# Softmax row sums of two attention layers: the partial sums are added and inverted when the next chunk but one begins, the product comes at its fifth unit, and the seventh head group takes no weight maxima

## The chip, the cores and the metric

The kernel runs on one core of a Trainium2 chip. The metric is the device time of one execution in microseconds, as the median of several runs. A core has TensorE (PE in the profile), VectorE (DVE), ScalarE (ACT), GpSimd (POOL) and SyncE (SP), each with a queue of its own that runs in order, and 16 DMA engines that the queues of SyncE and GpSimd feed here.

## What is computed

A sequence of 2048 positions with 1024 features goes through four layers, each added to its input: attention with 32 heads, a spectral filter, and both once more. The change lies in the attention layers.

```python
def _A_ref(x, wqkv, wo):
    B, S, D = x.shape
    H = 32
    Dh = D // H
    qkv = (lambda x, *d: x.transpose(*d))((x @ wqkv).reshape(B, S, 3, H, Dh), 2, 0, 3, 1, 4)
    q, k, v = qkv[0], qkv[1], qkv[2]
    scores = jnp.einsum("bhqd,bhkd->bhqk", q, k) * (Dh ** -0.5)
    p = _softmax(scores, axis=-1)
    o = jnp.einsum("bhqk,bhkd->bhqd", p, v)
    return (lambda x, *d: x.transpose(*d))(o, 0, 2, 1, 3).reshape(B, S, D) @ wo
...
x = x + _A_ref(_layernorm(x, axis=-1), A_wqkv, A_wo)
x = x + _B_ref(_layernorm(x, axis=-1), B_w_r, B_w_i)
```

`_B_ref` multiplies the two-dimensional Fourier transform of its input by a filter and transforms back.

## The kernel before

**Tiling.** The 32 heads form eight head groups `g` of four. A group takes its 2048 queries in four chunks `c` of 512, and a chunk takes the 2048 keys in sixteen units `kt` of 128. A unit (`S`, L714) makes the scores of four heads with twelve matmuls (L720) into two of the three PSUM tiles `s`; ScalarE writes two tiles `p` of exponentials (L724); VectorE adds them to the chunk's running sum `acc` (`add`, L737: L741 for the first two units together, L743 for each later one, two instructions a unit); TensorE multiplies them by the values (`PV`, L726: L730). Two chunks alternate between two tiles `acc`, one of which lies in the tensor `R`. There are eight buffers `p`. `PV` and the adds run one or two units behind the scores: at each even `kt` the loop does the products of the last two units, and the adds follow in that round and the next; at `kt == 0` both adds of the chunk before are done at once.

**Fill work.** Between the units TensorE computes the queries, keys and values of later groups (`qk_chunk`, L411, and `v_tiles`, L468) in small pieces, into a single PSUM bank `x`. ScalarE and VectorE then empty that bank: the high half of a split by L215, the low half by L216 on VectorE, or by L472 on ScalarE for values. The next sum can only start when the bank is empty. Norms of queries and keys bound the scores: `norms` (L437) takes one of the three tiles `s`, multiplies by ones (L443) and lets VectorE take the maximum (L445); GpSimd then makes the bias of the exponentials (L449 to L456, with a reduction over partitions, L451). In the last group but one the fill work ends with the splits of the output weights (`load_wo`), and in the last group it is the output projection (`wo_part`, L545: L531 into the bank `x`, emptied by L557 on VectorE).

**Row sums.** When a chunk's `acc` is complete, at `kt == 0` of the following chunk, `partials` (L746) puts seven DMAs on GpSimd's queue. Four add the four strips of 32 partitions into a DRAM tensor `zd` (L749), two fold that tensor in halves (L752), and one loads the remaining eight partial sums into `part` (L754). Each waits for the one before. `invert_partials` (L757) then has VectorE add the eight (L759), take the reciprocal (L761) and keep its maximum for a check (L762), and SyncE store it (`zr`, L764) and load it back spread over the partitions (`zt`, four DMAs, L766). `times` (L788: L789) multiplies the chunk's output `oc` by it, and `out` (L792) splits the product into halves (L795 on ScalarE, L796 on VectorE) and stores them (`od`, L798), from where `load_o` (L520) fetches them for the projection. The last group does the same without DMAs, with a matmul and transposes (`fin`, L769).

**Order.** The loop (L823 to L892) is written out by hand. TensorE and ScalarE run in the order written (`manual_schedule`, L823). VectorE, GpSimd and SyncE are ordered by a scheduler that follows the dependences; `issue_after` ties an instruction to a given add, so that it isn't moved ahead of it. In the first layer VectorE also takes the largest magnitude of each piece of the weights (`look`, L317: L320), once a chunk at `kt == 3`, tied to an add, and in the last group with every fourth unit, not tied.

Of the kernel before, what the change touches and what calls it, by code (L numbers as in the profile page):

```python
# [107 lines left out]
NG, NCH, NKT, NST = 8, 4, 16, 6  # L108
# [110 lines left out]
def run(g):  # L219
    for _ in g:  # L220
        pass
# [106 lines left out]
def attention(nc, tc, layer, ap, xin, yd, wts, wo, cst, dram, flags):  # L328
# [151 lines left out]
    def sums(ph):  # L480
        return 8 if ph[0] == "v" else 4
# [38 lines left out]
    def load_o(c):  # L520
        osb[c] = xhl[:, 2 + c % 2]
        for i in range(2):
            nc.sync.dma_start(osb[c][:, i, 0:7], od[i, 0:7, :, c * 512:(c + 1) * 512].rearrange("g p n -> p g n"))
# [21 lines left out]
    def wo_part(c, t, dst, nd):  # L545

        x = xres(c, t)
        st = sm.tile([128, 2, 6], F32, name="st")
        for n in range(2):
            p = bank()  # L550
            m = wo_mm(p, c, t, n, range(nd))
            for _ in range(3 * nd - 1):
                next(m)
                yield
            run(m)
            sl = slice(n * 512, n * 512 + 512)
            nc.vector.scalar_tensor_tensor(dst[:, sl], p, 1.0 / (SO * SW), x[:, sl], op0=ALU.mult, op1=ALU.add)  # L557
            if nd == 8:
                nc.vector.bn_stats(st[:, n], dst[:, sl])
                if n:  # L560
                    r0 = c * 512 + t * 128
                    nc.sync.dma_start(yd[r0:r0 + 128, :], dst)
                    nc.vector.bn_aggr(mvs[:, 8 * c + 2 * t:8 * c + 2 * t + 2], st)
            yield
# [16 lines left out]
    def wo_parts():  # L581
        load_o(0)
        for t in (2, 3, 0, 1, 4, 5, 6, 7, 8, 9, 10, 11):
            if t == 8:
                two = wvp.tile([128, 2, 1024], F32, name="wv")
                wo_dst[8], wo_dst[9] = two[:, 0], two[:, 1]
            yield from wo_part(t // 4, t % 4, wo_dst[t], 8 if t == 11 else 7)
            if t in (0, 4, 9):
                load_o({0: 1, 4: 2, 9: 3}[t])

    def wo_rest(t):
        p = psS.tile([128, 2, 512], F32, name="s")
        st = wo_last(t // 4, t % 4, p, wo_dst[t], wo_dst[t], True, t < 8)
        if t < 8:
            moments.extend((wo_mean, t) if i == 0 else (wo_var, t) for i in range(2))
        else:
            nc.vector.bn_aggr(mvs[:, 2 * t:2 * t + 2], st)
# [116 lines left out]
    def S(g, c, kt):  # L714

        s = [psS.tile([128, 2, 512], F32, name="s") for _ in range(2)]
        for i, (a, b) in enumerate(((0, 0), (0, 1), (1, 0))):
            for h in range(4):
                r = slice(32 * h, 32 * h + 32)
                nc.tensor.matmul(s[h // 2][:, h % 2], K[g][r, a, kt * 128:kt * 128 + 128],  # L720
                                 Q[g][r, b, c * 512:c * 512 + 512], start=i == 0, stop=i == 2)
        for hf in range(2):
            p = P[g, c, kt, hf] = pp.tile([128, 2, 512], F32, name="p")
            nc.scalar.activation(p, s[hf], AF.Exp, bias=bias[g], scale=SCALE / (SQ * SQ))  # L724
# [32 lines left out]
    def invert_partials(g, c, part):  # L757
        z = sm.tile([128, 16], F32, name="z")
        nc.vector.tensor_reduce(z, part.rearrange("p j q -> p q j"), axis=AX.X, op=ALU.add)  # L759
        rc = sm.tile([128, 16], F32, name="rc")  # L760
        nc.vector.reciprocal(rc, z)  # L761
        nc.vector.tensor_max(flags["r"], flags["r"], rc)  # L762
        r = on.tile([128, 512], F32, name="zt")
        nc.sync.dma_start(zr[c % 2].rearrange("(p q) -> p q", q=16), rc)  # L764
        for h in range(4):
            nc.sync.dma_start(r[32 * h:32 * h + 32], zr[c % 2][512 * h:512 * h + 512].unsqueeze(0).broadcast_to([32, 512]))  # L766
        return r
# [20 lines left out]
    def times(g, c, r):  # L788
        nc.vector.scalar_tensor_tensor(r, O[g, c], SO, r, op0=ALU.mult, op1=ALU.mult)  # L789
        O[g, c] = r  # L790

    def out(g, c, eng=nc.vector):  # L792
        r = O.pop((g, c))
        t = on2.tile([128, 2, 512], F16, name="ohl")
        nc.scalar.copy(t[:, 0], r)  # L795
        eng.tensor_tensor(t[:, 1], r, t[:, 0], op=ALU.subtract)  # L796
        if g < NG - 1:
            nc.sync.dma_start(od[:, g, :, c * 512:(c + 1) * 512].rearrange("a p n -> p a n"), t)  # L798
        else:
            olast[c] = t  # L800

    pend, done, late, going, turned = [], [], [], [], []
# [6 lines left out]
    def slots(f, sums, n, steps):  # L809

        while sums:
            k = max(1, int(n / sums + 0.5))
            m = -(-steps // k)
            for i in range(0, steps, m):
                while ripe():
                    norms()
                for _ in range(min(m, steps - i)):
                    next(f, None)
                n -= 1
                yield sums - (i + m >= steps)  # L820
            sums -= 1

    with tc.manual_schedule(engines={mybir.EngineType.PE, mybir.EngineType.Activation}):  # L823
        for g in range(NG):
            todo = sum(sums(ph) for ph in beside.get(g, []))
            sl = slots(fill, todo, 22 if g == NG - 2 else 32, 24)
            wsl = slots(wof, 4, 10, 21)
            for u in range(NCH * NKT):
                c, kt = divmod(u, NKT)
                S(g, c, kt)  # L830
                if g == u == 0:
                    run(last_v)
                if kt % 2 == 0:
                    for w in pend:
                        PV(*w)
                    late = pend
                    pend = []
                    if kt == 0 and late:
                        for w in late:
                            last_add = add(*w)  # L840
                        turned, going = going, []
                        if late[1][0] == NG - 1:
                            done = [late[1][:2]]
                            fin(*done[0])
                        else:
                            going = [*late[1][:2], partials(*late[1][:2])]
                        if turned and not done:
                            with tc.issue_after(last_add.ins):
                                times(*turned)
                        late = []  # L850
                for w in late[:1]:
                    last_add = add(*w)
                late = late[1:]
                if kt == 3 and u > 3:
                    with tc.issue_after(last_add.ins):
                        wts.look()
                if kt == 11 and going:
                    with tc.issue_after(last_add.ins):
                        going[2] = invert_partials(*going)
                if kt == 3 and turned and done:  # L860
                    with tc.issue_after(last_add.ins):
                        times(*turned)
                if kt == 5 and done:
                    out(*done.pop())
                elif turned and (kt == 5 or kt == 9):
                    out(*turned[:2])
                    turned = []
                pend.append((g, c, kt))
                if kt % 2 == 0:
                    continue  # L870
                if todo:
                    todo = next(sl)
                elif g == NG - 2:
                    if left:
                        run(lwo)
                        left = 0
                    if next(wsl, None) is not None and u == NCH * NKT - 1:
                        run(wsl)
                elif g == NG - 1:
                    if u % 4 == 1:  # L880
                        wts.look()
                    if moments:
                        f, t = moments.pop(0)
                        f(t)
                    if u // 2 in rests:
                        wo_rest(rests[u // 2])
                    for _ in range(share[u // 2]):
                        next(wof)
                if g == NG - 2 and todo <= 6 and left > (8 if todo > 4 else 0):
                    next(lwo)  # L890
                    left -= 1
        for w in pend:  # L892
            PV(*w)
        for w in late + pend:
            add(*w)
        run(wof)
# [580 lines left out]
```

## Time and profile before

| | us |
|---|---|
| median of 3 runs | 3784.86 |
| lowest and highest run | 3784.84, 3788.1 |
| the profiled execution | 3787.86 |
| its span, first to last instruction | 3786.0 |
| first layer's attention up to the last chunks | 110 to 1455 |
| second layer's | 1960 to 3330 |
| mean granted TensorE clock | 0.989 |

Times in profile rows are microseconds from the span's start. A row of the timeline gives start, duration, engine, line, operation, output and inputs, how many instructions it merges, and in brackets the idle time ahead of it with the engine, tile and line that ended it. A row of the waits names who waited, for whom, the total, how many times and the longest. A row of the windows gives the stretch, its length, the busy time of PE, PEld (the weight loads), DVE, ACT and POOL, then the granted clock of TensorE as a share of full speed, the share of DMA time and GB/s. TensorE is busy when its rows say so, even if the clock is lowered; its matmuls overlap.

### The profile page before, as it was taken

How to read it: one execution, taken by the hardware profiler on the slowest of the kernel's cores; microseconds unless marked ns; L12 is line 12 of the kernel's file. 1: busy time of each engine (PE TensorE's matmuls, PEld its weight loads, DVE VectorE, ACT ScalarE, POOL GpSimd, SP SyncE). 2: the span in 40 equal slices, each digit the busy share in tenths (PEclk: the TensorE clock that was granted, in tenths of full speed). 3: DMA queues.
4: the chain of work that ended last, by engine and by line, in shares of the span. 5: the costliest groups of instructions: out<-in, count | busy, mean ns of one | idle time of the engine just before them, and what ended most of it. 6: DMA issues, size and time to landing. Idle time of an engine off the chain costs nothing.

```text
span 3786.0 us, 80539 instructions
## 1 busy us (share of the span) xinstructions
PE 3658.5 (97%) x32919; PEld 1634.9 (43%) x32919; DVE 3132.8 (83%) x3800; ACT 2932.5 (77%) x3653; POOL 638.8 (17%) x798
## 2 busy tenths in 40 slices
PE   8999999999999999999999999999999999899998
PEld 5333422343234233378963234323433432233888
DVE  7799898989898978886767888989899888688744
ACT  5778887888788867768847788878888888577686
POOL 1011111111111110014420111111111111100143
PEclk9999999999999999999999999999999999999999
DMA  6122232322232442233151232323222333421423
GB/s 193 24 51 54 50 56 44 63 42 54 43 63 49 101 98 71 79 121 121 58 162 24 51 57 49 57 43 62 41 54 51 62 58 90 101 73 68 164 88 108
DMA packets 203551, 274.33 MB, mean 72 GB/s; under 512 B 75809, under 2 KB 122529, under 8 KB 202145
## 3 DMA queue, kind: packets, MB, share of 16 engines
q1 hardware_dynamic: 164208, 195.06, 16.2%
q0 software_dynamic: 37632, 73.43, 13.7%
q8 instruction: 260, 4.26, 0.5%
q14 instruction: 123, 1.00, 0.1%
q10 hardware_dynamic: 1328, 0.59, 0.1%
HBM read 149.00 MB, written 118.42 MB: 71 GB/s over the span
## 4 chain that ended last, share of the span: by engine, by line


## 5 line engine op out<-in xcount | busy, mean ns | idle before, releaser
L724 ACT ACTIVATE p<-s,bias 128x1024 f32<-128x1024 f32 x2048 | 2169.5, 1111 | 553.8 <-PE s L720 532.1
L743 DVE TENSOR_TENSOR R<-R,p 128x1024 f32<-128x1024 f32 x896 | 1044.3, 1219 | 65.4 <-ACT p L724 63.7
L743 DVE TENSOR_TENSOR acc<-acc,p 128x1024 f32<-128x1024 f32 x896 | 1043.8, 1218 | 60.3 <-ACT p L724 58.7
L730 PE MATMUL o<-p,R 128*32 128x512 f32 x8192 | 987.1, 599 | 0.0
L411 PE MATMUL x<-big,wqk 128*128 128x512 f16 x2880 | 686.4, 384 | 37.7 <-DVE R L216 30.5
L720 PEld LDWEIGHTS <-R 32*128 32x128 f16 x12288 | 229.5, 92 | 758.0 <-issue 642.5
L411 PEld LDWEIGHTS <-wqk 128*128 128x128 f16 x3072 | 279.3, 98 | 460.1 <-issue 174.3
L730 PEld LDWEIGHTS o<-p,R 128*32 128x32 f32 x8192 | 214.1, 109 | 526.1 <-issue 526.1
L720 PE MATMUL s<-R 32*128 32x512 f16 x6144 | 428.7, 379 | 7.1 <-DVE mqk L445 6.8
L720 PE MATMUL s<-Q,R 32*128 32x512 f16 x6144 | 425.6, 377 | 9.8 <-DVE mqk L445 9.8
L468 PE MATMUL x<-wv,big 128*128 128x256 f16 x2784 | 332.1, 275 | 6.6 <-DVE R L216 4.8
L468 PEld LDWEIGHTS <-big 128*128 128x128 f16 x3072 | 292.0, 99 | 98.4 <-issue 56.5
L531 PE MATMUL x<-big 128*128 128x512 f16 x1008 | 235.7, 384 | 17.8 <-DVE R L557 17.8
L531 PEld LDWEIGHTS <-big 128*128 128x128 f16 x1428 | 135.3, 98 | 185.0 <-issue 50.6
L749 POOL DMA_DIRECT2D zd<-R x112 | 93.3, 833 | 706.3 <-DVE R L743 427.8
L749 POOL DMA_DIRECT2D zd<-acc x112 | 92.3, 824 | 709.3 <-DVE acc L743 428.7
L741 DVE SCALAR_TENSOR_TENSOR R<-p 128x1024 f32<-128x1024 f32 x64 | 75.5, 1221 | 99.0 <-ACT p L724 99.0
L752 POOL DMA_DIRECT2D zd<-zd x112 | 89.3, 798 | 397.6 <-DMA zd<-zd 174.7
L1141 DVE TENSOR_TENSOR H<-G,H 128x512 f16<-128x512 f32 (+1 forms) x68 | 46.7, 687 | 99.6 <-ACT H L1140 99.4
L741 DVE SCALAR_TENSOR_TENSOR acc<-p 128x1024 f32<-128x1024 f32 x64 | 75.8, 1221 | 44.1 <-ACT p L724 44.1
L1083 ACT COPY U<-ps 64x256 f32<-64x256 f32 (+1 forms) x272 | 97.0, 357 | 8.7 <-PE ps L1090 3.6
L1090 PE MATMUL ps<-cbi,H 128*128 128x256 f16 (+1 forms) x792 | 99.0, 273 | 3.4 <-DVE H L1141 1.9
(459 smaller groups left out, 3294.1 us busy)
## 6 DMA issues: line engine op xcount, KB each, us to landing
zd<-R POOLq DMA_DIRECT2D x112, 256.0 KB, 4.1
zd<-acc POOLq DMA_DIRECT2D x112, 256.0 KB, 4.1
wst<-in_wp SPq DMA_DIRECT2D x96, 256.0 KB, 3.5
R<-y SPq DMA_DIRECT2D x32, 512.0 KB, 6.0
w<-in_w SPq DMA_DIRECT2D x60, 256.0 KB, 2.7
zt<-zr SPq DMA_DIRECT2D x224, 64.0 KB, 2.0
od<-ohl SPq DMA_DIRECT2D x56, 256.0 KB, 2.7
big<-od SPq DMA_DIRECT2D x16, 896.0 KB, 6.9
```

Of the source, the lines that this page charges most:

```text
L411: nc.tensor.matmul(ps, a, b, start=i == 0, stop=i == 23)
L468: nc.tensor.matmul(ps[:, j], x[c][:, d, o:o + 128], w[:, n, d], start=i == 0, stop=i == 23)
L531: nc.tensor.matmul(p, a, b, start=start and d == ds[0] and i == 0, stop=stop and d == ds[-1] and i == 2)
L720: nc.tensor.matmul(s[h // 2][:, h % 2], K[g][r, a, kt * 128:kt * 128 + 128], Q[g][r, b, c * 512:c * 512 + 512], start=i == 0, stop=i == 2)
L724: nc.scalar.activation(p, s[hf], AF.Exp, bias=bias[g], scale=SCALE / (SQ * SQ))
L730: nc.tensor.matmul(O[g, c][32 * h:32 * h + 32], V[g][:, kt, 32 * h:32 * h + 32], P[g, c, kt, h // 2][:, h % 2], start=kt == 0, stop=kt == ...
L741: last_add = nc.vector.scalar_tensor_tensor(a, P[g, c, 0, hf], 1e-34, p, op0=ALU.add, op1=ALU.add)
L743: last_add = nc.vector.tensor_add(a, a, p)
L749: nc.gpsimd.dma_start(z, a[32 * j:32 * j + 32].rearrange("p a j n -> p (a j n)"), max_dma_last_dim=2048, **({"accum_op": ALU.add} if j els ...
L752: nc.gpsimd.dma_start(z[0:n], z[n:2 * n], accum_op=ALU.add, max_dma_last_dim=2048)
L1083: nc.scalar.copy(ov[64 * r:64 * r + 64, a0:a0 + m, x], tl[64 * x:64 * x + 64, :m, r])
L1090: nc.tensor.matmul(out, l, r, start=k == 0, stop=k == len(mm_) - 1)
```

## The change

The diff, cut to its core:

```diff
-            if t in (0, 4, 9):
-                load_o({0: 1, 4: 2, 9: 3}[t])
+            if t in (0, 5, 9):
+                load_o({0: 1, 5: 2, 9: 3}[t])
...
                             going = [*late[1][:2], partials(*late[1][:2])]
-                        if turned and not done:
+                        if turned:
                             with tc.issue_after(last_add.ins):
-                                times(*turned)
+                                turned[2] = invert_partials(*turned)
                         late = []
...
-                if kt == 3 and u > 3:
+                if kt == 3 and u > 3 and g < NG - 2:
                     with tc.issue_after(last_add.ins):
                         wts.look()
-                if kt == 11 and going:
-                    with tc.issue_after(last_add.ins):
-                        going[2] = invert_partials(*going)
-                if kt == 3 and turned and done:
+                if kt == 5 and done:
+                    out(*done.pop())
+                if kt == 5 and turned:
                     with tc.issue_after(last_add.ins):
                         times(*turned)
-                if kt == 5 and done:
-                    out(*done.pop())
-                elif turned and (kt == 5 or kt == 9):
+                if kt == 7 and turned:
                     out(*turned[:2])
                     turned = []
```

For a chunk that ends when the following one begins, `invert_partials` moved from unit 11 of the following chunk to the first unit of the chunk after that; `times` moved from that first unit to unit 5, `out` from unit 5 to unit 7. The third load of the output halves moved from behind the projection's fifth tile to behind its sixth. The weight maxima tied to unit 3 are dropped in the last two groups, so that those pieces are left to the untied ones of the last group. Nothing is computed differently. The orders of TensorE and GpSimd are the same as before.

The second half of the fifth head group's last chunk on VectorE. Before (`acc` is the running sum, `R` here the keys, `wqk` the next weights):

```order
L796 TENSOR_TENSOR ohl<-zt,ohl 128x512
L216 SCALAR_TENSOR_TENSOR R<-x,R 128x512
L422 TENSOR_TENSOR sq<-R 128x512
L743 TENSOR_TENSOR acc<-acc,p 128x1024 x4
L216 SCALAR_TENSOR_TENSOR wqk<-wst,wqk 128x512 x2
L743 TENSOR_TENSOR acc<-acc,p 128x1024 x4
L759 TENSOR_REDUCE z<-part 128x16
L761 RECIPROCAL rc<-z 128x16
L762 TENSOR_TENSOR fr<-fr,rc 128x16
L743 TENSOR_TENSOR acc<-acc,p 128x1024 x4
L216 SCALAR_TENSOR_TENSOR R<-x,R 128x512
```

And now, up to the next chunk's first adds:

```order
L743 TENSOR_TENSOR acc<-acc,p 128x1024 x4
L796 TENSOR_TENSOR ohl<-zt,ohl 128x512
L216 SCALAR_TENSOR_TENSOR wqk<-wst,wqk 128x512 x2
L743 TENSOR_TENSOR acc<-acc,p 128x1024 x8
L216 SCALAR_TENSOR_TENSOR R<-x,R 128x512
L422 TENSOR_TENSOR sq<-R 128x512
L743 TENSOR_TENSOR acc<-acc,p 128x1024 x8
L759 TENSOR_REDUCE z<-part 128x16
L761 RECIPROCAL rc<-z 128x16
L216 SCALAR_TENSOR_TENSOR R<-x,R 128x512
L422 TENSOR_TENSOR sq<-R 128x512
L762 TENSOR_TENSOR fr<-fr,rc 128x16
```

The three instructions of the reciprocal left the middle of the chunk and stand at its end, around a split of the keys; the subtraction L796 moved down, directly ahead of the weights' splits.

The seventh head group's second chunk on VectorE in the first layer, from its first adds (`big` holds the output weights). Before:

```order
L741 SCALAR_TENSOR_TENSOR acc<-p 128x1024 x2
L216 SCALAR_TENSOR_TENSOR R<-x,R 128x512
L216 SCALAR_TENSOR_TENSOR big<-wst,big 128x512
L320 TENSOR_REDUCE fw<-wqk 128x1
L743 TENSOR_TENSOR acc<-acc,p 128x1024 x2
L320 TENSOR_REDUCE fw<-big 128x1
L743 TENSOR_TENSOR acc<-acc,p 128x1024 x2
L216 SCALAR_TENSOR_TENSOR big<-wst,big 128x512
L743 TENSOR_TENSOR acc<-acc,p 128x1024 x4
L796 TENSOR_TENSOR ohl<-zt,ohl 128x512
L216 SCALAR_TENSOR_TENSOR big<-wst,big 128x512
L320 TENSOR_REDUCE fw<-big 128x1
```

Now:

```order
L741 SCALAR_TENSOR_TENSOR acc<-p 128x1024 x2
L216 SCALAR_TENSOR_TENSOR R<-x,R 128x512
L216 SCALAR_TENSOR_TENSOR big<-wst,big 128x512
L320 TENSOR_REDUCE fw<-big 128x1
L743 TENSOR_TENSOR acc<-acc,p 128x1024 x4
L216 SCALAR_TENSOR_TENSOR big<-wst,big 128x512
L789 SCALAR_TENSOR_TENSOR zt<-oc,zt 128x512
L743 TENSOR_TENSOR acc<-acc,p 128x1024 x4
L216 SCALAR_TENSOR_TENSOR big<-wst,big 128x512
L320 TENSOR_REDUCE fw<-big 128x1
L743 TENSOR_TENSOR acc<-acc,p 128x1024 x4
L796 TENSOR_TENSOR ohl<-zt,ohl 128x512
```

The tied maximum of `wqk` is gone from here, but untied maxima of `big` that belong to the last group stand in this group before and now.

SyncE's queue in the first head groups (`zr` and `zt` are the reciprocals' store and loads, `wst` the weights of later groups). Before:

```order
L764 DMA zr_1130<-rc 128x16
L766 DMA zt<-zr_1130 32x512 x4
L798 DMA od_132<-ohl 128x2x512
L764 DMA zr_1131<-rc 128x16
L766 DMA zt<-zr_1131 32x512 x4
L302 DMA wst<-in_wp 128x512 x4
```

Now:

```order
L764 DMA zr_1130<-rc 128x16
L766 DMA zt<-zr_1130 32x512 x4
L798 DMA od_132<-ohl 128x2x512
L302 DMA wst<-in_wp 128x512 x2
L764 DMA zr_1131<-rc 128x16
L766 DMA zt<-zr_1131 32x512 x4
L302 DMA wst<-in_wp 128x512 x2
```

Two of the weights' loads moved ahead of the store of a reciprocal.

## The prediction

> **What bounds the kernel now.** I read the page's first part, then the waits of the matmul queue (PE) in the two attention stages, then VectorE's (DVE's) waits there.
>
> ```profile
> span 3786.0 us, 80539 instructions
> PE 3658.5 (97%) x32919; PEld 1634.9 (43%) x32919; DVE 3132.8 (83%) x3800; ACT 2932.5 (77%) x3653; POOL 638.8 (17%) x798
> ```
>
> TensorE is busy for 97% of the span, so what it loses sets the time. Its waits of the first layer's attention (110 to 1455 us), then of the second's (1960 to 3330 us):
>
> ```profile
> PE x L411 <- DVE R L216: 18.6, 7, 7.3
> PE x L531 <- DVE R L557: 8.1, 1, 8.1
> PE s L720 <- DVE mqk L445: 7.8, 6, 2.5
> PE x L411 <- DVE Q L216: 4.4, 3, 3.4
> PE x L468 <- DVE R L216: 2.6, 3, 0.9
> ...
> PE x L411 <- DVE R L216: 11.9, 5, 6.1
> PE x L531 <- DVE R L557: 9.6, 1, 9.6
> PE s L720 <- DVE mqk L445: 8.8, 5, 3.3
> PE x L411 <- DVE Q L216: 1.0, 1, 1.0
> ```
>
> The columns are the total in us, the number of waits and the longest. All are waits for VectorE to empty a PSUM buffer: 41.5 us in the first layer and 31.3 in the second, 72.8 us in 32 waits. VectorE's own waits, first layer and second:
>
> ```profile
> DVE z L759 <- DMA part<-zd: 39.7, 20, 9.6
> ...
> DVE z L759 <- DMA part<-zd: 39.8, 20, 11.2
> ```
>
> VectorE stands still for 79.5 us in 40 of 56 chunks because the sum of the partial row sums (L759) comes up before its DMA has landed. The fifth head group's last chunk shows how the one makes the other; GpSimd (POOL), DVE and PE in turn:
>
> ```profile
> 949.65 4.63 POOL L451 PARTITION_ALL_REDUCE mall<-mqk  x1 [11.20 <-DVE mqk L445]
> ...
> 962.90 0.76 POOL L749 DMA_DIRECT2D zd<-R  x1
> ...
> 987.42 0.99 POOL L754 DMA_DIRECT2D part<-zd  x1 [2.25 <-DMA zd<-zd]
> ...
> 980.28 4.62 DVE L743 TENSOR_TENSOR acc<-acc,p 128x1024 f32<-128x1024 f32 x4
> 992.40 0.37 DVE L759 TENSOR_REDUCE z<-part 128x16 f32<-128x128 f32 x1 [7.50 <-DMA part<-zd]
> 992.80 0.25 DVE L761 RECIPROCAL rc<-z 128x16 f32<-128x16 f32 x1
> 993.09 0.17 DVE L762 TENSOR_TENSOR fr<-fr,rc 128x16 f32<-128x16 f32 x1
> ...
> 997.72 0.68 DVE L216 SCALAR_TENSOR_TENSOR R<-x,R 128x512 f16<-128x512 f32 x1
> ...
> 985.89 1.90 PE L411 MATMUL x<-big,wqk 128*128 128x512 f16 x8
> ...
> 998.45 3.90 PE L411 MATMUL x<-big,wqk 128*128 128x512 f16 x10 [7.29 <-DVE R L216]
> ```
>
> GpSimd was still at the bias maximum when the chunk's sums were ready, so the chain of seven DMAs began at 962.9 and ended near 991. VectorE waited 7.50 us, the split L216 behind it came late, and TensorE waited 7.29 us for that split's PSUM bank.
>
> **Part 1, the wait at L759.** The trio L759, L761, L762 moves from behind the adds of unit 9 of the following chunk to behind its last adds, six units later. Two units are four adds, 4.62 us by the row at 980.28, so the trio comes 13.9 us later or more. The longest wait is 11.2 us, so all 40 should go, 79.5 us of VectorE. GpSimd's order is unchanged, and so is TensorE's. What is late next is VectorE's plain backlog, and three groups of TensorE's waits are that already. The three L468 waits (2.6 us) stand at a chunk's start, with no wait for a partial sum before them. Three L445 waits of 1.5 to 1.6 us stand in chunks like the one from 325 to 369 us; of this chunk the first row below tells, with its window. The rest are in the first layer's seventh head group (1233 to 1330 us), its three rows and a window of its first chunk:
>
> ```profile
> PE s L720 <- DVE mqk L445: 1.5, 1, 1.5
> ...
> 325.00:369.00 44.00, 41.63 (x404) 14.85 (x406) 41.83 (x44) 36.82 (x40) 6.97 (x8) 1.00 0.34 67
> ...
> PE x L411 <- DVE Q L216: 3.4, 1, 3.4
> PE s L720 <- DVE mqk L445: 2.5, 1, 2.5
> PE x L411 <- DVE R L216: 1.5, 2, 0.9
> ...
> 1233.00:1279.00 46.00, 42.05 (x371) 12.73 (x373) 45.63 (x49) 39.34 (x46) 5.40 (x7) 0.96 0.38 87
> ```
>
> The windows give PE busy first and DVE busy third. In the one chunk VectorE works for 41.83 us where TensorE needs 41.63; in the other it is full, 45.63 of 46.0. I leave 2.6 + 3 x 1.53 + 7.4 = 14.6 us in place, so 72.8 - 14.6 = 58.2 us of waits go.
>
> **Part 2, what moves into other waits.** Each chunk still does the trio (0.37 + 0.25 + 0.17 = 0.8 us), the product L789 and the subtraction L796, at other places. The subtraction (its times in ns are min, median and max):
>
> ```profile
> L796 DVE TENSOR_TENSOR ohl<-zt,ohl x64: 678/684/687, 210.0 to 3498.1; 128x512 f16<-128x512 f32 x64
> ```
>
> Where one of them now stands just ahead of a split or maximum that TensorE wants, the split is 0.68 us later. By the order this happens two or three times in a pair of head groups: the subtraction now runs directly ahead of a split of Q or the weights, and the trio ahead of a chunk's first adds and split. No row gives the price of such a place. The bounds are all 32 waits at 0.8 us, 25.6 us lost, and a gain of the 14.6 us above where the trio left a full stretch. I take 15 places at 0.68 us, 10.2 us, nearer the loss since VectorE is as full as TensorE in the window at 325. Left: 58.2 - 10.2 = 48.0 us.
>
> **Part 3, the clock after a wait.** The third figure from a window's end is the granted clock. Of ten windows of 20 us, one around each wait of 2.4 us or more, five stand at 0.91, four at 0.83 and one at 0.74; four of them, and a window around a 1.5 us wait:
>
> ```profile
> 262.00:282.00 20.00, 17.61 (x147) 5.32 (x146) 15.79 (x19) 12.59 (x13) 1.75 (x2) 0.91 0.19 43
> ...
> 985.00:1005.00 20.00, 12.71 (x104) 3.95 (x100) 11.08 (x14) 8.74 (x10) 1.16 (x2) 0.83 0.09 21
> ...
> 1306.00:1326.00 20.00, 17.47 (x150) 4.93 (x148) 17.34 (x20) 11.97 (x13) 0.98 (x1) 0.91 0.35 116
> ...
> 3234.00:3254.00 20.00, 10.36 (x79) 2.88 (x71) 11.60 (x13) 6.05 (x6) 1.77 (x2) 0.74 0.11 21
> ...
> 350.00:370.00 20.00, 17.64 (x192) 7.92 (x189) 18.88 (x21) 13.90 (x16) 3.69 (x5) 1.00 0.12 23
> ```
>
> So a wait costs more than itself: 0.09 x 20 = 1.8, 3.4 or 5.2 us of clock, 27.8 us in all if every one fell on work. Part falls on the wait: at 998.45 ten matmuls took 3.90 us where eight took 1.90, which is 1.5 us lost of that window's 3.4. I take 1.5 for each of the five long ones and 1.8 for each short one, 16.5 us, less the two short ones in the seventh head group, which stay: 12.9 us. The bounds are 0 (waits of 2 to 3 us remain and still lower it) and 27.8.
>
> The Trainium skill, TensorE: Matmul & The Clock Gate, Part 1 (The HAM clock gate), says that the clock halves after an idle window of about 3.4 us. The trace disagrees a little: waits of 2.4 us (the window at 262) and 2.5 us (at 1306) were enough, and 1.5 us was not. By the page the waits of 2.4, 2.5, 3.3 and 3.4 us would be free, and the sum would have 9.3 us in place of 12.9.
>
> **Part 4, the weight maxima.** One maximum takes 1.21 us:
>
> ```profile
> L320 DVE TENSOR_REDUCE fw<-wqk x16: 1207/1210/1215, 69.6 to 1284.2; 128x1 f32<-128x1024 f16 x16
> ```
>
> The maxima of the last head group are tied to no add, and VectorE's order puts them early: nine stand between the seventh group's adds before, eight now, and two more in the sixth group. One less is 1.2 us in a full stretch; I count 0, with 1.2 either way. The later load of the second output chunk has about two chunks' slack.
>
> **Sum.** 48.0 + 12.9 = 60.9 us. The profiled execution took 3787.86 us, 1.9 over its span, and 3.0 over the median of the runs, 3784.86. From it the sum gives 3727.0; from the median **3724 us**, which I forecast.
>
> **The rivals.** *VectorE takes over as the bound.* With its waits gone it has little idle left in chunks like that at 325, and half of the sum returns: 30.5 us saved, 3754 us. For it speaks 41.83 against 41.63; against it that only the first layer's chunks with a weight maximum look so. Chance 0.12.
>
> *The reciprocals come back too late (slower).* From trio to product there were twelve adds, now there are six, at 4.62 / 4 = 1.16 us about 6.9 us. SyncE's rows for one round trip, the landing of its last loads (min, median, max), and its longest kind of wait for a buffer:
>
> ```profile
> 1366.47 0.33 SPq L764 DMA_DIRECT2D zr<-rc  x1
> 1367.89 1.72 SPq L766 DMA_DIRECT2D zt<-zr  x4
> ...
> DMA to landing us min/median/max: 1.8/2.0/3.4
> ...
> SPq L302 <- DVE wqk L216: 501.3, 52, 56.2
> ```
>
> The trip is 1.42 + 1.72 + 2.0 = 5.1 us. It decides from 6.9 us on: a trip of 10 us, behind a weight load in SyncE's queue that waits for its buffer, would stop VectorE 56 times for 3.1 us, 174 us; at the ratio of now, 58.2 / 79.5, TensorE loses 127 us, and the time is 3724 + 127 = 3851 us. Against it: in the new order no load ahead of a reciprocal's store waits for a split behind that trio. Chance 0.03.
>
> *No change.* TensorE meets VectorE's backlog in the same places and the waits only change their releaser: 3785 us. Against it, the 7.50 and 7.29 us are one wait. Chance 0.03.
>
> *All of it goes.* No place in part 2 costs anything and the seventh group's waits go with it: 72.8 - 2.6 - 4.6 = 65.6, and 16.5 of clock, 82.1 us: 3703 us. Chance 0.10.
>
> **How the numbers follow.** The forecast has 0.72. Its own ends are 58.2 - 25.6 + 5 = 37.6 us saved, 3747 us, and 82 us saved. The range from 3706 to 3744 us leaves out the outer part of each and most of the first and second rivals, about 0.2. A measurement of this kernel can tell 0.2%, 7.6 us, from no change; the forecast, the first and the last rival are all faster by more, 0.94, and the other two hold 0.03 each.
>
> **What would show it.** In the changed kernel's profile VectorE's wait for the partial sums at L759 should be gone; TensorE's waits for L216, L557 and L445 in the attention stages should sum to about 25 us, most of them in the first layer and none over 4 us; the mean granted clock should rise above 0.989. I am wrong if L789 shows a wait for its DMA of over 1 us in most chunks, if TensorE's waits fall by less than 35 us, or if the clock stays low without long waits.

## The result and the profile after

| | median us | lowest to highest | ratio to before, 95% interval |
|---|---|---|---|
| before, in the same session | 3784.85 | 3781.26 to 3788.1 | |
| changed | 3717.1 | 3715.37 to 3718.52 | 0.9821, 0.9804 to 0.9838 |

The change saves 67.8 us by the medians. The forecast was 3724.0 us, 6.9 us too high and inside the range. The profiled execution of the changed kernel took 3715.37 us, 1.9 over its span, so the spans differ by 3786.0 - 3713.5 = 72.5 us; its mean granted clock is 0.996 (0.989 before).

The first part of the page of the changed kernel:

```profile
span 3713.5 us, 80684 instructions
PE 3642.4 (98%) x32919; PEld 1630.7 (44%) x32919; DVE 3134.8 (84%) x3800; ACT 2930.9 (79%) x3653; POOL 629.0 (17%) x798
```

VectorE does the same 3800 instructions in nearly the same busy time (3132.8 us before), and TensorE the same 32919 in 16.1 us less (3658.5 before). TensorE's waits in the changed kernel, first layer's attention, then second's:

```profile
PE x L411 <- DVE Q L216: 4.5, 4, 2.7
PE x L468 <- DVE R L216: 4.4, 3, 1.5
PE s L720 <- DVE mqk L445: 1.6, 3, 0.9
PE x L411 <- DVE R L216: 1.2, 1, 1.2
...
PE x L468 <- DVE R L216: 1.0, 3, 0.3
```

The waits for L216, L557 and L445 sum to 11.7 us in the first layer and 2.2 in the second (the row shown, 1.0, and 0.5, 0.4 and 0.3), 13.9 us where they were 72.8; both waits at L531 (8.1 and 9.6 us before) are gone, and nothing is over 2.7 us. VectorE's longest group of waits in the whole run, changed kernel, is one for the exponentials:

```profile
DVE R L741 <- ACT p L724: 101.2, 29, 16.4
```

The wait for `part` (L759), 79.5 us before, is not in that list any more, and no wait of L789 for `zt` has come in its place.

The stages say where the 72.5 us came from. The windows of the two attention stages, each from and to the same place in the work, before:

```profile
110.00:1455.00 1345.00, 1303.22 (x12136) 458.02 (x12138) 1189.96 (x1229) 1082.47 (x1153) 196.26 (x224) 0.99 0.29 57
1960.00:3330.00 1370.00, 1338.17 (x12424) 483.06 (x12422) 1167.36 (x1209) 1089.78 (x1168) 198.06 (x232) 0.99 0.29 59
```

And changed:

```profile
110.00:1418.00 1308.00, 1295.22 (x12133) 455.69 (x12135) 1190.35 (x1231) 1081.41 (x1153) 193.44 (x224) 1.00 0.29 58
1923.00:3259.05 1336.05, 1332.15 (x12424) 481.78 (x12422) 1167.67 (x1208) 1089.32 (x1168) 191.95 (x232) 1.00 0.30 61
```

The stages are 37 and 34 us shorter. TensorE's idle time in them, length less busy, fell from 41.8 to 12.8 and from 31.8 to 3.9 us, 56.9 us in all; its busy time fell by 8.0 + 6.0 = 14.0 us with equal work, which fits the slow matmuls behind the long waits. The two make up the 71 us, and the rest of the program is about 1.5 us shorter.

At the place that the prediction showed, the fifth head group's last chunk, GpSimd, VectorE and TensorE in the changed kernel:

```profile
945.40 0.76 POOL L749 DMA_DIRECT2D zd<-R  x1
...
969.66 0.99 POOL L754 DMA_DIRECT2D part<-zd  x1 [2.85 <-DVE acc L743]
...
976.72 0.69 DVE L216 SCALAR_TENSOR_TENSOR R<-x,R 128x512 f16<-128x512 f32 x1
...
977.65 4.63 DVE L743 TENSOR_TENSOR acc<-acc,p 128x1024 f32<-128x1024 f32 x4
...
987.89 0.36 DVE L759 TENSOR_REDUCE z<-part 128x16 f32<-128x128 f32 x1
...
978.30 2.76 PE L411 MATMUL x<-big,wqk 128*128 128x512 f16 x12
```

The last DMA of the chain is issued at 969.66, as before some 24 us after the first, and L759 reads its result 18.2 us later without a bracket, that is, without idle time ahead of it. The split of the keys at 976.72 stands behind adds without a stop, and the matmuls that fill the bank next start without idle time: twelve take 2.76 us, where before ten took 3.90 after a wait of 7.29.

### The profile page after: what moved, and what is told of

It reads as the page before. It is cut to its first block, busy times and chain, and to the rows that moved or that the text cites. A ratio compares the mean times of both kernels' runs of the same rounds, so it can differ in the third digit from the quotient of the medians.

```text
span 3713.5 us, 80684 instructions
## 1 busy us (share of the span) xinstructions
PE 3642.4 (98%) x32919; PEld 1630.7 (44%) x32919; DVE 3134.8 (84%) x3800; ACT 2930.9 (79%) x3653; POOL 629.0 (17%) x798
## 3 DMA queue, kind: packets, MB, share of 16 engines
q1 hardware_dynamic: 164208, 195.06, 16.5%
## 4 chain that ended last, share of the span: by engine, by line
## 5 line engine op out<-in xcount | busy, mean ns | idle before, releaser
L743 DVE TENSOR_TENSOR acc<-acc,p 128x1024 f32<-128x1024 f32 x896 | 1045.9, 1223 | 61.1 <-ACT p L724 58.2
L411 PE MATMUL x<-big,wqk 128*128 128x512 f16 x2880 | 677.7, 381 | 8.1 <-DVE Q L216 4.8
L468 PE MATMUL x<-wv,big 128*128 128x256 f16 x2784 | 329.6, 274 | 9.5 <-DVE R L216 7.7
L468 PEld LDWEIGHTS <-big 128*128 128x128 f16 x3072 | 291.0, 98 | 99.8 <-issue 59.3
L531 PE MATMUL x<-big 128*128 128x512 f16 x1008 | 231.9, 380 | 0.0
L749 POOL DMA_DIRECT2D zd<-R x112 | 93.3, 833 | 697.4 <-DVE z L759 288.7
L531 PEld LDWEIGHTS <-big 128*128 128x128 f16 x1428 | 134.4, 98 | 164.6 <-issue 29.2
L749 POOL DMA_DIRECT2D zd<-acc x112 | 92.4, 825 | 670.4 <-DVE z L759 324.7
```

The source lines that it names most:

```text
L411: nc.tensor.matmul(ps, a, b, start=i == 0, stop=i == 23)
L468: nc.tensor.matmul(ps[:, j], x[c][:, d, o:o + 128], w[:, n, d], start=i == 0, stop=i == 23)
L531: nc.tensor.matmul(p, a, b, start=start and d == ds[0] and i == 0, stop=stop and d == ds[-1] and i == 2)
L743: last_add = nc.vector.tensor_add(a, a, p)
L749: nc.gpsimd.dma_start(z, a[32 * j:32 * j + 32].rearrange("p a j n -> p (a j n)"), max_dma_last_dim=2048, **({"accum_op": ALU.add} if j els ...
```

## The experiments

The theory is that VectorE's wait for `part` at L759 is the whole cause: it holds the splits and maxima behind it, TensorE stops for them, and the clock falls after the longer stops. The rivals are that the new order of VectorE brings the gain whatever L759 does, that the maxima carry it, and that a wait moved to L789 would cost as much as one at L759, or would be absorbed. Kernels of one session ran on the same chip; the three sessions had different ones, and the time of the kernel before is given for each.

**First session** (before: 3782.39 us, 3777.99 to 3790.47).

*A shorter chain, the order as before.* Against the kernel before:

```diff
-        for j in range(4):
+        for j in range(2):
             nc.gpsimd.dma_start(z, a[32 * j:32 * j + 32]...
```

> The kernel before, with every instruction of VectorE, TensorE and ScalarE in its old place, but two of the four strips' DMAs of each chunk left out of the row sums (so half of each row sum is missing from the output). The chain on GpSimd is then some 9 us shorter and ends before unit 9 of the next chunk. If the wait for the partial sums is the cause, VectorE's 79.5 us at L759 fall to under 5, TensorE's waits on VectorE in the attention stages from 72.8 to under 20 us, the mean granted clock rises from 0.989 to 0.995 or more, and the time is that of the changed kernel, 3717 us, within 8. If the new places of the instructions are what helped (rival), the time stays within 20 us of 3785.

Measured: 3715.96 us (3712.89 to 3717.1), ratio 0.9823 (0.9806 to 0.9839), clock 0.995. The wait at L759 is left in two chunks. Its row and those of TensorE's waits for L557, L445 and L216, over the whole run:

```profile
DVE z L759 <- DMA part<-zd: 9.0, 2, 7.0
...
PE x L531 <- DVE R L557: 6.0, 2, 5.5
PE s L720 <- DVE mqk L445: 5.4, 9, 0.9
PE x L468 <- DVE R L216: 4.8, 4, 2.2
...
PE x L411 <- DVE Q L216: 3.4, 1, 3.4
PE x L411 <- DVE R L216: 2.7, 3, 1.1
```

The 9.0 us are more than the 5 expected: at 1332.1 and 3174.3 us, late in the seventh head group of each layer, even the short chain ends too late, and TensorE's longest wait, at L531, stands behind the first of the two. In the attention stages TensorE's waits for VectorE sum to 20.1 us, just over the 20 expected.

So with the order of before, and most of the wait taken away at its source, 66.4 us go, against 67.8 in the changed kernel. The wait is the cause, and the new order as such brings nothing that can be measured. Since the short chain is as fast with 9.0 us of the wait left, the new order may cost a few us of its own; part 2 below shows where.

*The product two units earlier.* Against the changed kernel:

```diff
-                if kt == 5 and turned:
+                if kt == 3 and turned:
                     with tc.issue_after(last_add.ins):
                         times(*turned)
```

> The changed kernel with the product L789 at unit 3 in place of unit 5: two adds in place of six between the reciprocal and the product. The round trip over DRAM takes 1.4 + 1.7 + 2.0 to 2.8 us, so VectorE should wait at L789 1.5 to 3.5 us in most of the 56 chunks, 80 to 200 us in all. If TensorE only loses what stands right ahead of a split or maximum that it needs (my theory), the time rises by 15 to 50 us, to 3732 to 3767 us. If every us of VectorE's waiting costs TensorE 0.73 us (the ratio that I took for the slow rival), it rises by 60 to 145 us, to 3777 to 3862 us.

Measured: 3815.69 us (3806.84 to 3819.12), ratio 1.0081 (1.0063 to 1.0099): slower than before. VectorE's longest group of waits, and TensorE's:

```profile
DVE zt L789 <- DMA zt<-zr: 123.0, 46, 4.9
```

```profile
PE x L411 <- DVE Q L216: 28.2, 13, 6.9
PE x L468 <- DVE R L216: 27.4, 7, 5.2
PE s L720 <- DVE mqk L445: 15.0, 9, 3.5
...
PE s L443 <- DVE sq L422: 12.2, 4, 3.8
```

VectorE waits 2.7 us on average in 46 chunks, and it costs 3815.69 - 3717.1 = 98.6 us over the changed kernel's first measurement (beside which the kernel before differed by 2.5 us from the one here), 0.80 us for each us waited. That is in the second of the two ranges (3777 to 3862 us); my theory, that TensorE loses only what stands right ahead of a split or maximum that it needs, gave 3732 to 3767 us and is refuted. A wait at L789 costs nearly what one at L759 does, 67.8 / 79.5 = 0.85. The six adds that the change leaves between reciprocal and product are enough; two units fewer are not.

*The reciprocal two units earlier.* Against the kernel before:

```diff
-                if kt == 11 and going:
+                if kt == 9 and going:
                     with tc.issue_after(last_add.ins):
                         going[2] = invert_partials(*going)
```

> The kernel before with the sum of the partial sums two units earlier, at unit 9 in place of 11. Each of the 56 chunks then waits 4.6 to 5.2 us longer, so VectorE's wait at L759 rises from 79.5 us to 320 to 370 us. If waits this long reach TensorE nearly whole and lower its clock (my theory), it loses 250 us or more in waits and some 60 to 90 us in clock over the changed kernel: 4000 to 4080 us. If TensorE loses 0.73 of each us and the clock adds little, the time is 3717 + 0.73 x 345 = 3950 to 3990 us.

Measured: 4045.23 us (4038.55 to 4051.9), ratio 1.0696 (1.0671 to 1.0721), clock 0.957. VectorE and TensorE:

```profile
DVE z L759 <- DMA part<-zd: 340.2, 54, 15.5
```

```profile
PE x L411 <- DVE R L216: 101.8, 20, 6.5
PE s L720 <- DVE mqk L445: 80.2, 16, 7.2
```

This is what my theory expected. The cost over the changed kernel is 328 us for 340.2 us waited, 0.96 us each; over the short chain, which has the same order, it is 329 us for 331 us more. The edit leaves the chain of DMAs as it is, so the price is that of the wait, and not of the traffic that the short chain saves too. The cost of the wait goes with its length from 0 over 79.5 to 340 us, and with each step the clock goes down: 0.996, 0.989, 0.957.

**Second session** (before: 3768.55 us, 3760.77 to 3780.13). These four edits, and those of the third session, are edits of the changed kernel.

*The maxima kept in the last groups*, so that only the places of reciprocal and product differ from before:

```diff
-                if kt == 3 and u > 3 and g < NG - 2:
+                if kt == 3 and u > 3:
```

> The changed kernel with the weight maxima of the last two head groups tied to unit 3 again, as before the change. VectorE's order then has nine maxima among the seventh group's adds, in place of eight. If this part of the change is worth what I counted, nothing or one maximum, the time is 3715 to 3720 us, the same as the changed kernel. If the maxima behind the second chunk's first adds are what filled VectorE there (rival), TensorE's longest wait in the seventh group grows from 2.7 to 3.4 us or more and the clock halves once or twice more: 3721 to 3726 us.

Measured: 3716.2 us (3712.61 to 3717.66), ratio 0.9859 (0.9839 to 0.9879). TensorE's waits for the queries' split in the first layer:

```profile
PE x L411 <- DVE Q L216: 5.4, 4, 3.6
```

The longest wait is 3.6 us where the changed kernel has 2.7, the sign that the rival named, but the time lies between the two medians that the changed kernel had elsewhere, 3717.1 and 3714.33 us. The part of the change that concerns the maxima is worth nothing that can be measured.

*All maxima tied to adds*, those of the last group too, so that the seventh takes three of them and not eight:

```diff
-                if kt == 3 and u > 3 and g < NG - 2:
+                if kt == 3 and u > 3 and g < NG - 1:
...
                     if u % 4 == 1:
-                        wts.look()
+                        with tc.issue_after(last_add.ins):
+                            wts.look()
```

> The changed kernel with the untied maxima of the last head group tied to the add of their unit, so that they stay in that group; three tied ones remain in the seventh. VectorE then has three maxima there in place of eight. If the maxima are what keeps TensorE waiting in the seventh group of the first layer (2.7 + 1.2 + 0.9 + 0.6 us, and 1.7 us of clock), 4 to 7 us go: 3710 to 3713 us. If the splits of the output weights fill VectorE there by themselves (rival), the time stays at 3715 to 3720 us.

Measured: 3711.71 us (3711.18 to 3713.8), ratio 0.9849 (0.983 to 0.9869). The first layer's longest wait for the queries is now short:

```profile
PE x L411 <- DVE Q L216: 3.2, 4, 1.4
```

It is 4.5 us under the kernel that kept the maxima, with ranges that overlap a little. Fewer maxima in the seventh head group may bring something; the change took away one of nine, since the untied ones still come there.

*The subtraction two units later.* In the changed kernel L796 stands directly ahead of a split at some places, and this moves it:

```diff
-                if kt == 7 and turned:
+                if kt == 9 and turned:
                     out(*turned[:2])
```

> The changed kernel with the split of the product at unit 9 in place of 7. VectorE's subtraction L796 then stands ahead of no split of queries, keys or values. If a subtraction right ahead of such a split costs TensorE its 0.6 us, the waits of 0.6 us for L216 at 215, 568 and 921 us go and the three of 1.5 us fall back to 0.9, some 4 us: 3711 to 3715 us. If VectorE's backlog at those places only shifts to the next split (rival), the time stays at 3715 to 3720 us.

Measured: 3708.52 us (3707.87 to 3708.72), ratio 0.984 (0.982 to 0.9859). Its first layer has these waits for VectorE:

```profile
PE s L720 <- DVE mqk L445: 3.9, 6, 1.5
PE x L411 <- DVE R L216: 3.3, 2, 2.1
PE x L468 <- DVE R L216: 2.6, 3, 0.9
PE x L411 <- DVE Q L216: 2.4, 1, 2.4
```

The three waits at L468 are back at the 2.6 us of before, and of the four for the queries' split one is left. Others grew, so that the waits of this layer sum to about as much. The time is 7.7 us under the kernel that kept the maxima, more than was expected. By its page TensorE's busy time is 3638.6 us, 3.8 less than in the changed kernel. Some 1.4 us of that can be read: its longest wait, 2.42 us at 1227.41, is followed by eight matmuls in 1.89 us, where the changed kernel's of 2.69 us is followed by eight in 3.27. The rest stays open.

*Both*, the ties and the subtraction at unit 9:

> Both of the two before: the last group's maxima tied, and the split of the product at unit 9. If both gains are real and lie at different waits they add up, 8 to 11 us: 3706 to 3711 us. If TensorE's remaining waits are one backlog that moves on, no more than the better of the two goes.

Measured: 3708.08 us (3705.99 to 3710.0), ratio 0.9839 (0.9819 to 0.9859). This lies in the range for gains that add, but only because the subtraction alone brought more than expected: it is 0.4 us under that, so the gains do not add. In the first layer the projection now waits for the output halves, which the later subtraction stores later:

```profile
PE x L531 <- DMA big<-od: 2.9, 1, 2.9
```

**Third session** (before: 3768.31 us, 3758.49 to 3778.83).

*The changed kernel again*, with no edit:

> The changed kernel itself, as the measure for the kernels that run beside it. The kernel before took 3785 us beside its first runs and 3769 us beside the last ones; the waits that it has and the changed kernel has not depend on how long the DMAs of the partial sums take. If that is the whole difference, the changed kernel is again at 3715 to 3719 us, whatever the kernel before takes here; if the chips differ as such, both move together.

Measured: 3714.33 us (3712.02 to 3715.19), ratio 0.9855 (0.983 to 0.988). The changed kernel differs by 2.8 us from its first measurement, and the kernel before by 16.5, so the change saves 54.0 us here where it saved 67.8.

*Both edits again*, the same kernel as above:

> The kernel with tied maxima and the split of the product at unit 9, beside the changed kernel on one chip: 8 to 10 us under it, 3706 to 3710 us, if the gain is real; within 3 us of it if the earlier difference was one between chips.

Measured: 3708.75 us (3706.8 to 3710.74), ratio 0.9841 (0.982 to 0.9863), 5.6 us under the changed kernel beside it, less than expected.

*The subtraction at unit 9 only in the first six head groups*, with the ties, so that the projection finds its halves in time:

```diff
-                if kt == 7 and turned:
+                if kt == (9 if g < NG - 2 else 7) and turned:
                     out(*turned[:2])
```

> As the kernel with tied maxima and the split at unit 9, but with the split at unit 7 again in the last two head groups, whose output halves are loaded back at once. There the split at 9 made TensorE wait 2.9 us in the first layer and 1.2 us in the second for the load of the output halves. If those waits are the cost of the later store, they go and 3 to 5 us are won over it, 3702 to 3706 us; if the subtractions of the last groups stand ahead of splits again, as much is lost as is won, and the time stays at 3706 to 3710 us.

Measured: 3703.99 us (3702.42 to 3706.39), ratio 0.983 (0.9809 to 0.9852), 10.3 us under the changed kernel and 4.8 under the version with unit 9 throughout, as expected. The first layer's waits for VectorE:

```profile
PE x L468 <- DVE R L216: 2.6, 3, 0.9
PE s L720 <- DVE mqk L445: 2.4, 5, 0.6
PE x L411 <- DVE Q L216: 1.4, 1, 1.4
```

This is the fastest version, 64.3 us under before on its chip.

*The reciprocal only two units later than before*, at unit 13, with the product where the changed kernel has it:

```diff
-                        if turned:
-                            with tc.issue_after(last_add.ins):
-                                turned[2] = invert_partials(*turned)
...
+                if kt == 13 and going:
+                    with tc.issue_after(last_add.ins):
+                        going[2] = invert_partials(*going)
```

> The changed kernel with the sum of the partial sums at unit 13 of the following chunk, two units later than before and four earlier than the change puts it. Only the five waits for partial sums of over 4.6 us are left, those whose chain of DMAs begins behind GpSimd's bias maximum (or, in two, is long), each shorter by 4.6 to 5.2 us: 15 us of VectorE's waiting in all, and nearly as much of TensorE's, with three or four spells of lowered clock, 5 us. Time 3730 to 3740 us. If short and long waits count alike and most of the gain comes with the five long ones (rival), more is lost: 3745 us or more; if VectorE absorbs what is left, 3717 to 3722 us.

Measured: 3724.93 us (3720.31 to 3725.77), ratio 0.9882 (0.986 to 0.9904), clock 0.994. VectorE's wait:

```profile
DVE z L759 <- DMA part<-zd: 8.8, 2, 4.6
```

Two units later take away nearly all of the wait: it is left once in each layer, late in the seventh head group (at 1340.0 and 3186.6 us), and the time is 10.6 us over the changed kernel's, below the 3730 to 3740 us expected and above the 3717 to 3722 of a wait that is absorbed. I had expected more waits, counted from the profile of before, which was taken in another session. That 8.8 us waited and 10.6 us lost are near each other is in part chance: TensorE's waits behind the two, at L531, are 2.49 and 2.83 us, and the rest of the loss is not traced.

## Why the prediction held, step by step

**Part 1, the wait at L759: right.** All of it went, GpSimd and TensorE kept their order, and the short chain shows that nearly all of this alone is worth the time.

**Part 1, what stays: too much.** I left 14.6 us in place. The L468 waits stayed (2.6 us; they stand in the middle of a chunk, some 20 us behind its first adds, not at its start), and of the seventh head group's 7.4 us 4.8 are left (its window in the prediction is that of the second chunk, not of the first). The three L445 waits, 4.6 us that I put down to plain backlog, went. The chunk from 325 to 369 us of the kernel before shows what they were:

```profile
357.19 0.37 DVE L759 TENSOR_REDUCE z<-part 128x16 f32<-128x128 f32 x1 [0.67 <-DMA part<-zd]
...
360.24 0.68 DVE L445 TENSOR_REDUCE mqk<-s 128x1 f32<-128x512 f32 x1
...
360.98 0.82 PE L720 MATMUL s<-Q,R 32*128 32x512 f16 x10 [1.50 <-DVE mqk L445]
```

L759 waited 0.67 us there and the trio took 0.8, two adds ahead of the maximum, 1.47 us in all, and TensorE's wait is 1.50. In the two other such chunks L759 waited 0.71 and 0.70 us (at 719 and 1083 us), for TensorE's 1.55 and 1.53. So the short wait at L759 made about half of it, and the trio, in the way of the maximum, the other half. The short chain shows this: it has no wait at L759 there and the trio in its old place, and TensorE's waits at these three places are 0.73, 0.73 and 0.74 us. The window, with VectorE busy for 41.83 of 44 us, hid it.

**Part 2, the moved instructions: the price was right, the count was not.** I took 15 places at 0.68 us, 10.2 us. Outside the seventh head group nine have a price, six in the first layer at 0.6 us and three in the second at about half of that. One of each kind of the first layer in the changed kernel, VectorE first:

```profile
214.71 0.69 DVE L796 TENSOR_TENSOR ohl<-zt,ohl 128x512 f16<-128x512 f32 x1
215.31 0.69 DVE L216 SCALAR_TENSOR_TENSOR Q<-x,Q 128x512 f16<-128x512 f32 x1
...
216.06 2.75 PE L411 MATMUL x<-big,wqk 128*128 128x512 f16 x12 [0.61 <-DVE Q L216]
...
347.38 0.69 DVE L796 TENSOR_TENSOR ohl<-zt,ohl 128x512 f16<-128x512 f32 x1
347.98 0.69 DVE L216 SCALAR_TENSOR_TENSOR R<-x,R 128x512 f16<-128x512 f32 x1
...
348.72 1.91 PE L468 MATMUL x<-wv,big 128*128 128x256 f16 x16 [1.47 <-DVE R L216]
```

Three waits of 0.61 us are new (at 215, 568 and 921), and the three at L468 grew from 0.87 to 1.47 us (at 347, 700 and 1053): 3 x 0.61 + 3 x 0.60 = 3.6 us. In the second layer, where no weight maxima are taken, the same subtraction makes three new waits at L468 of 0.34 to 0.35 us (at 2201, 2552 and 2903), 1.0 us. The count from the order took every place where a moved instruction stands ahead of a split. In the changed kernel the subtraction stands directly ahead of a split of queries or keys at sixteen places outside the seventh head group; at the seven others TensorE waits 0.2 us or not at all. That the price depends on whether VectorE is late there already fits the rows, but no run varies it alone. By the terms of the prediction: 13.9 = 2.6 + 4.8 + 3.6 + 1.0 us and 1.9 of small waits are left where I expected 14.6 + 10.2 = 24.8, so 58.9 us went for 48.0. Here lies most of the forecast's miss: the loss was put at 15 full prices, and 7.2 of the 14.6 us did not stay.

**Part 3, the clock: right, 1.1 us too small.** TensorE's busy time in the two stages fell by 14.0 us for 12.9; the other 2.1 us of the 16.1 lie outside them. The seventh head group's longest wait still lowers the clock in the changed kernel, by a window around it and TensorE's rows:

```profile
1222.00:1242.00 20.00, 17.31 (x148) 5.15 (x144) 20.00 (x21) 15.19 (x19) 2.95 (x4) 0.91 0.39 81
```

```profile
1228.62 1.17 PE L720 MATMUL s<-R 32*128 32x512 f16 x12
1232.47 3.27 PE L411 MATMUL x<-big,wqk 128*128 128x512 f16 x8 [2.69 <-DVE Q L216]
```

Eight matmuls take 3.27 us behind a wait of 2.69 where eight take 1.90 elsewhere, 1.4 us lost, near the 1.5 that I took. The Trainium skill, TensorE: Matmul & The Clock Gate, Part 1 (The HAM clock gate), gives an idle window of about 3.4 us; the measurement decides, and here 2.69 us were enough, as 2.4 and 2.5 us were before. But the length of the wait alone does not decide it, as the last section shows, so the prediction's line between 1.5 and 2.4 us is that of one profile.

**Part 4, the maxima: right.** Counted at 0, and the run that keeps them shows no difference.

**The sum.** 58.9 + 14.0 = 72.9 us for the 60.9 forecast. The spans show 72.5: TensorE's idle time in the stages fell by 56.9, not 58.9, since short waits for ScalarE and gaps without a releaser are about 2 us more, and 1.5 us went outside the stages. The medians show less than the spans, 67.8, since the profiled execution of before was 3.0 above its median and that of the changed kernel 1.7 below its own. So the terms missed by 12 us, and it is luck that the time missed by only 6.9. Luck too is the chip: where the kernel before takes 3768 us, the same change saves 54.

**The rivals.** *VectorE as the bound* is refuted: it is busy for 1190 of 1308 us in the first stage, TensorE for 1295, and the waits for VectorE that are left are 13.9 us. *The reciprocals too late* did not happen, but the run with the product at unit 3 shows the mechanism at its place, with the end on the other side: two units of lead decide it. Its price was too low: I took 0.73 us of TensorE's time for each us that VectorE waits, which is idle time alone; 0.80 and 0.96 were measured with the clock in it, and 58.2 + 16.5 over 79.5 is 0.94 by the prediction's own terms. *No change* is refuted by the medians. *All of it goes*, 3703 us, did not come, for the 4.6 us of part 2 and the 4.8 us of the seventh head group; the version with the ties and the subtraction at unit 9 in the early groups, which takes most of these away, comes to 3704 us.

## What to carry to other kernels

Where an engine that runs in order waits for a chain of DMAs, count who is queued behind the waiting instruction: with the one PSUM bank that stands between two engines here, nearly all of the wait reached the engine that bounds the kernel (0.80 to 0.96 us for each us; no run has a second bank), and moving the reader two units later gave 43 of the 54 us that six units later gave on that chip, with equal instructions. Then look for the next latency on the same path (here the reciprocals' trip, which two units less of lead made worth 98.6 us) before you move it further. An order shows where instructions meet, and only the windows of the trace show whether the meeting costs; here a moved instruction cost nearly its own duration at six of sixteen such places, and at the others less or nothing.

## What the runs showed of the hardware

The lowered clock is 14.0 of the 71 us by which the two stages became shorter. How long a wait must be is not a fixed number here. It was lowered after waits of 2.39 and 2.53 us before and 2.69 us in the changed kernel, but not after 2.42 us with the subtraction at unit 9. Two more cases, from the changed kernel measured again (granted clock 0.91 from 1268 to 1288 us) and from the reciprocal at unit 13 (1.00 from 3187 to 3207):

```profile
1276.45 0.82 PE L720 MATMUL s<-R 32*128 32x512 f16 x10 [0.63 <-ACT p L724]
1278.58 4.41 PE L411 MATMUL x<-big,wqk 128*128 128x512 f16 x12 [1.31 <-DVE R L216]
...
3197.23 4.69 PE L531 MATMUL x<-big 128*128 128x512 f16 x21 [2.83 <-DVE R L557]
```

In the first, twelve matmuls take 4.41 us behind stops of 0.63 and 1.31 us; at the same place of the changed kernel's first profile, behind 0.63 and 1.21 us, twelve take 2.75. In the second, 21 matmuls run at full rate behind 2.83 us (21 take 4.71 us elsewhere). What else decides it, these runs do not show.

The small loads that spread the reciprocals take longer when they are asked for at another place. The landing of `zt`'s loads, in the changed kernel (1.8, 2.0 and 3.4 us before):

```profile
DMA to landing us min/median/max: 1.9/2.8/4.8
```

The kernel before took 3785 and 3782 us in two sessions and 3768 in the two others, on other chips; the changed kernel 3717 and 3714. Only the kernel that waits for the DMA chain differs. From the first L749 to L754, over the chunks, the chain takes 24.4 us in the median and 29.0 at most in the profile of before. In the changed kernel, whose chain is the same, it takes 24.4 and 28.6 in its first profile and 24.1 and 26.5 on the last chip, 0.48 us less in the mean. Times the 40 chunks that wait and the 0.85 us lost for each us, that is an estimate of 16 us, the size of the difference between the chips. That the faster chain there is what makes the kernel before faster also fits the fewer waits with the reciprocal at unit 13, but no profile of the kernel before was taken on that chip, so it is not shown.
